# Order of vector work in the first steps of an up-projection: product of g ahead of the weight conversions, a normalisation split in two

## The chip, the cores and the metric

One core of a Trainium2 chip runs the whole program in one launch. The metric is the device time of that launch in microseconds. Three executions of the kernel before took 534.69, 539.32 and 541.73 us; the median, 539.32 us, is what the change is compared with.

The core has four compute engines that matter here, each with its own queue that is worked off in order: PE (TensorE, matrix products), DVE (VectorE), ACT (ScalarE) and POOL (GpSimd). SP (SyncE) issues the transfers. PE writes to PSUM banks; VectorE and ScalarE read them.

## The reference, cut to what matters

```python
attn_out = softmax(scale * q @ k.T + decay, causal) @ v       # 4 batches, 8 heads, 576 tokens, 64 wide
x = attn_out.transpose(0, 2, 1, 3).reshape(2304, 512)
h = x @ w_in                                                  # 512 -> 2048, the up-projection
g = h * (1.0 / (1.0 + np.exp(-h)))
x = g @ w_out
...                                                           # a soft mixture of 8 experts on x
```

The inputs w_in and w_out are float64 in the host's arrays; the kernel reads them as pairs of 32-bit words and turns them into float32 itself.

## The kernel before, in words

The program has three stages: attention (to about 190 us of the profile), the up-projection with everything that hangs on it (about 190 to 480 us), and the tail with the experts.

**The up-projection.** The 2304 tokens are nine chunks of 256 tokens (NCH = 9), the 2048 columns are four groups of 512 (fg = 0 to 3). A step k is one chunk with one group. The first 16 steps take four chunks (NJ = 4) under each group in turn: steps 0 to 3 are group 0, 4 to 7 group 1, and so on; from step 16 the chunks come one after the other. A step has two halves t = 0 and 1 of 128 tokens. Each half is one accumulation of 12 matmuls of 128x512 in one PSUM bank (`h_part`, lines 583 to 601; x and w are each a high and a low part, so lines 593, 594 and 595 follow each other four times). The banks of h are a ring of three (`RINGS["h"] = "014"`): a half can only begin when the half three before it has been read for the last time.

After a half, ScalarE takes its tanh from PSUM (`g_tanh`, line 607, tile gt), and VectorE multiplies (tanh + 1) by h from PSUM (`g_mul`, line 614). This **product of g** is the last reader of the bank, so it is what PE waits for three halves later: the half t = 1 of step k needs the product of the half t = 0 of step k - 1.

**The conversions.** Beside this, VectorE, ScalarE and GpSimd convert the weights that later steps need. A weight block (128x512, tile raw) takes five VectorE instructions (`conv_b` line 486, `conv_d` lines 496, 498, 500, 502), two or three of ScalarE (lines 489, 509, 513) and one or two of GpSimd (line 520 for w_in, lines 524 and 525 for w_out). Blocks go in pairs, so a pair is ten VectorE instructions. `conv_ops(n)` issues from a list (`CQ`, built by `front` and `back`) until n VectorE instructions are out, with those of ScalarE and GpSimd that stand between them. It is called with OPS = 4 twice in every step: between the tanh and the product of the first half, and at the end of the step (one more call ahead of step 0 finds no block to work on). When a pair of w_out is done, its transposes and products (`w_prime_a`, `w_prime_b`, `w_prime_c`, tiles wtp, wp1, wp2) follow on PE in later steps.

**The last normalisation.** The attention output of the last pair of heads is still to be divided by its row sums when the up-projection starts. `norm_b` and `norm_x` (end of step 0) invert the sums, write them to device memory (R) and read them back spread over the partitions (RB, line 334). `norm_c` (lines 338 to 343) then does three VectorE instructions: 128x256 for chunk 6, 128x256 for chunk 7, 128x64 for chunk 8. It stands at the end of step 3. Chunks 6 to 8 are needed much later.

The order on each engine is the order in which the Python code issues (the schedule is manual), so moving a call moves its instructions in the queue.

Of the kernel before, what the change touches and what calls it, by code (L numbers as in the profile page):

```python
# [35 lines left out]
def tile_attention_moe_softmoe(ctx: ExitStack, tc: tile.TileContext, qk, vr, f, wcat, phi, w1, w2, out):  # L36
# [298 lines left out]
                              in_=bass.AP(tensor=r.tensor, offset=r.offset + h * S, ap=[[0, 64], [1, S]]))  # L335
        RT[p] = rb

    def norm_c(p):
        b, hp = divmod(p, NP)
        u, r = U.pop(p), RT.pop(p)  # L340
        for x, c0, n in ((xs[2 * b][:, hp], 0, 256), (xs[2 * b + 1][:, hp], 256, 256),
                         (xs[8][:, hp, 64 * b:64 * b + 64], 512, 64)):
            nc.vector.tensor_tensor(x, u[:, c0:c0 + n], r[:, c0:c0 + n], ALU.mult)

    def att_step(i, cv):
# [206 lines left out]
    def conv_ops(n):  # L552
        while n > 0:
            if not CQ or CQ[0] is None:
                m = mo["todo"]
                more = mo["next"] >= m + 2 and sent[m + 1] + LAG <= mo["k"]
                if CQ:
                    CQ.pop(0)
                    if more:
                        CQ[0:0] = front(m)  # L560
                        CQ.extend(back(m))
                        mo["todo"] += 2
                    continue
                if not more:
                    return
                CQ.extend(front(m) + back(m))
                mo["todo"] += 2
            v, fn, m = CQ.pop(0)
            n -= v
            fn(m)  # L570
# [14 lines left out]
    def h_part(c, fg, t, d0, d1):  # L585
        xh, xl = XC[c]
        if d0 == 0:
            G[c, fg, t] = bank("h", [128, 512], "h")
        o = G[c, fg, t]
        tok = slice(128 * t, 128 * t + 128)  # L590
        for d in range(d0, d1):
            w = W[4 * fg + d]
            nc.tensor.matmul(o, lhsT=xh[:, d, tok], rhs=w[:, 0], start=(d == 0), stop=False)  # L593
            nc.tensor.matmul(o, lhsT=xl[:, d, tok], rhs=w[:, 0], start=False, stop=False)  # L594
            nc.tensor.matmul(o, lhsT=xh[:, d, tok], rhs=w[:, 1], start=False, stop=(d == 3))  # L595
        if t == 1:
            if c == NCH - 1:
                release(*WS[fg][d0:d1])
            if fg == 3 and d1 == 4:
                release(*XS[c])  # L600

    def g_tanh(c, fg, t, parts=1):
        if (c, fg) not in GT:
            GT[c, fg], GS[c, fg] = page([128, 2, 512], "gt")
        n = 512 // parts
        for j in range(parts):
            nc.scalar.activation(GT[c, fg][:, t, n * j:n * j + n], G[c, fg, t][:, n * j:n * j + n], AF.Tanh, scale=0.5)  # L607

    def g_mul(c, fg, t, parts=1):
        n = 512 // parts  # L610
        h = G.pop((c, fg, t))
        for j in range(parts):
            g = GT[c, fg][:, t, n * j:n * j + n]
            nc.vector.scalar_tensor_tensor(g, g, 1.0, h[:, n * j:n * j + n], op0=ALU.add, op1=ALU.mult)  # L614
# [364 lines left out]
    with tc.manual_schedule():  # L979
# [156 lines left out]
        for k, (c, fg) in enumerate(steps):  # L1136
            last = k == len(steps) - 1
            mo["k"] = k
            if k == NJ * 4:
                RINGS.update(h="01", t="254")  # L1140
            if k == STEPS[1]:
                RINGS.update(t="25", g="b4")
            mo["cap"] = [n for at, n in CAPS if k >= at][-1]
            if c == NCH - 1:
                h_part(c, fg, 0, 0, 2)
                h_part(c, fg, 1, 0, 2)
                stacked(k)
                square(k)
                h_part(c, fg, 0, 2, 4)
                g_tanh(c, fg, 0)  # L1150
                g_mul(c, fg, 0)
                h_part(c, fg, 1, 2, 4)
            else:
                h_part(c, fg, 0, 0, 4)
                g_tanh(c, fg, 0)
                conv_ops(OPS)
                g_mul(c, fg, 0)
                halfway(k)
                h_part(c, fg, 1, 0, 4)
            if c in (0, 1) and fg == 0:  # L1160
                split_x(c + 2)
            elif NJ <= c < NCH - 1 and fg == 1:
                split_x(c + 1)
            elif (c, fg) == (NJ - 1, 3):
                split_x(NJ)
            g_tanh(c, fg, 1, 1 + last)
            g_mul(c, fg, 1, 1 + last)
            born[c, fg] = k
            if k == 0:
                norm_b(NPAIR - 1)  # L1170
                norm_x(NPAIR - 1)
            if k == 3:
                norm_c(NPAIR - 1)
                release((xpool, "x1"), (nrm, "U1"), (nrm, "R"))
            if c < NCH - 1:
                stacked(k)
                square(k)
                conv_ops(OPS)
            elif fg != 2:
                stacked(k + 0.5)  # L1180
                if fg == 1:
                    square(k + 0.5)
            if last:
                ct_page(0)
                ct_page(4)
            mo["umax"] = max([0] + [n for at, n in ROOM if k + 1 >= at])
            pump()
# [52 lines left out]
```

## Time and profile before

| | |
|---|---|
| median of three executions | 539.32 us (534.69 to 541.73) |
| profiled execution, its own time | 539.69 us |
| span in the profile, first to last instruction | 538.0 us |
| granted TensorE clock, mean over the span | 0.988 |
| busy share of the span | PE 95%, weight loads 70%, VectorE 62%, ScalarE 55%, GpSimd 39% |

The profile is of one execution. Its times are microseconds from the span's start. The busy shares are averages over stages of very different kind; what the first steps of the up-projection cost has to be read in the stretch from 190 to 300 us. In a row of the timeline, a number in square brackets is the idle time of the engine just before, and behind the arrow stands what ended it.

### The profile page before, as it was taken

To read this page: it belongs to the slowest core of one execution; us is meant where nothing else is said; L and a number is where in the kernel's file an instruction comes from. 1 tells how busy PE (TensorE), PEld (TensorE's weight loads), DVE (VectorE), ACT (ScalarE), POOL (GpSimd) and SP (SyncE) were. 2 spreads that over 40 slices of the span, in tenths; PEclk is the share of its full clock that TensorE was granted. 3 is DMA by queue.
4 is the path that set the end of the run, shared out by engine and by line. 5 is a ranking of instruction groups with operands and counts; after the bars stand their busy time and mean duration, and the time that the engine had idled before them with its cause. 6 is when DMAs were issued, how large, how long until landed. Compare 5 with 4: busy or idle time off the path is not lost.

```text
span 538.0 us, 11312 instructions
## 1 busy us (share of the span) xinstructions
PE 510.0 (95%) x4167; PEld 375.0 (70%) x4167; DVE 332.5 (62%) x891; ACT 296.8 (55%) x585; POOL 208.6 (39%) x228
## 2 busy tenths in 40 slices
PE   8799999999999999899999999999998999999993
PEld 4587787778777777677776777667675667665562
DVE  5747677767789389998888733566654431434023
ACT  8678989888896766456656553323421333341013
POOL 9757888888788404457357300000000000001000
PEclk9989999999999999899999999999999999999997
DMA  5716765576473377212431209789698829767998
GB/s 144 216 66 167 207 197 162 147 216 175 119 191 79 127 295 308 111 40 78 158 100 58 80 1 334 215 240 291 225 340 203 256 69 337 248 256 303 409 396 303
DMA packets 43820, 105.81 MB, mean 197 GB/s; under 512 B 8148, under 2 KB 16628, under 8 KB 43764
## 3 DMA queue, kind: packets, MB, share of 16 engines
q1 hardware_dynamic: 43764, 105.08, 59.8%
q8 instruction: 33, 0.54, 0.4%
q14 instruction: 23, 0.19, 0.1%
HBM read 82.58 MB, written 17.52 MB: 186 GB/s over the span
## 4 chain that ended last, share of the span: by engine, by line
PE 66%; DVE 11%; DMA 9%; ACT 6%; issue 3%; POOL 2%; SPq 1%; DVEq 0%; POOLq 0%; ACTq 0%
PE h L593 9%; PE h L595 8%; PE h L594 8%; PE av L303 4%; PE st L246 4%; PE mx L200 4%; DMA QA<-mr 4%; PE gtp L637 4%; PE st L248 3%; PE lp L664 3%; PE rs L287 3%; PE so L906 3%; PE h L851 3%; PE pp L780 2%; PE st L89 2%
## 5 line engine op out<-in xcount | busy, mean ns | idle before, releaser
L593 PE MATMUL h<-w,xh 128*128 128x512 f32 x288 | 119.3, 414 | 3.7 <-DVE gt L614 3.6
L595 PE MATMUL h<-w,xh 128*128 128x512 f32 x288 | 114.3, 397 | 0.0
L594 PE MATMUL h<-w,xl 128*128 128x512 f32 x288 | 114.1, 396 | 0.0
L614 DVE SCALAR_TENSOR_TENSOR gt<-gt,h 128x512 f32<-128x512 f32 (+1 forms) x73 | 48.4, 674 | 70.0 <-ACT gt L607 70.0
L607 ACT ACTIVATE gt<-h 128x512 f32<-128x512 f32 (+1 forms) x73 | 42.7, 589 | 85.0 <-PE h L595 71.4
L252 ACT ACTIVATE E<-st 128x256 f32<-128x256 f32 (+4 forms) x160 | 63.6, 431 | 15.0 <-PE st L248 12.5
L206 DVE CUSTOM_DVE_ANT_0 junk<-mx,mask 128x64 bf16<-128x64 f32 (+3 forms) x128 | 50.0, 414 | 33.7 <-PE mx L200 32.8
L593 PEld LDWEIGHTS h<-w,xh 128*128 128x128 f32 x288 | 54.6, 189 | 21.4 <-DVE gt L614 7.0
L826 POOL MEMSET SM<- 128x512 f32 x2 | 1.1, 530 | 175.9 <-ACT gt L607 173.3
L595 PEld LDWEIGHTS h<-w,xh 128*128 128x128 f32 x288 | 54.5, 189 | 12.9
L594 PEld LDWEIGHTS h<-w,xl 128*128 128x128 f32 x288 | 54.5, 189 | 11.1
L246 PE MATMUL st<-QA,KA 128*128 128x256 f32 (+2 forms) x192 | 56.4, 304 | 6.0 <-DMA QA<-mr 4.1
L269 POOL TENSOR_SCALAR_AFFINE_SELECT E<-E 128x256 f32<-128x256 f32 (+1 forms) x96 | 41.8, 450 | 28.7 <-ACT E L252 27.3
L248 PE MATMUL st<-QB,KB 128*128 128x256 f32 (+2 forms) x192 | 52.5, 298 | 0.0
L200 PE MATMUL mx<-KA,QA 127*128 127x64 f32 (+2 forms) x192 | 50.6, 330 | 1.8 <-DVE mr L221 0.6
L303 PE MATMUL av<-E,VF 128*64 128x320 f32 (+4 forms) x448 | 50.8, 364 | 0.0
L178 POOL TENSOR_TENSOR QB<-qk,QA 64x576 fp32r<-64x576 f32 x30 | 42.8, 1428 | 2.3
L176 POOL TENSOR_TENSOR KB<-qk,KB 64x576 fp32r<-64x576 f32 x30 | 42.3, 1430 | 1.7 <-ACT KB L170 0.6
L246 PEld LDWEIGHTS st<-QA,KA 128*128 128x128 f32 x192 | 35.1, 183 | 10.6 <-ACT E L252 7.0
L303 PEld LDWEIGHTS av<-E,VF 128*64 128x64 f32 x448 | 29.5, 136 | 17.8 <-POOL E L269 0.3
L524 POOL TENSOR_TENSOR raw<-raw 128x512 f32<-128x512 f32 x16 | 25.4, 1590 | 38.8 <-ACT raw L513 31.8
L200 PEld LDWEIGHTS mx<-KA,QA 127*128 127x128 f32 x192 | 33.4, 192 | 5.9 <-DVE Mt L206 1.8
(155 smaller groups left out, 847.9 us busy)
## 6 DMA issues: line engine op xcount, KB each, us to landing
unit<-in_w_dram SPq DMA_DIRECT2D x64, 512.0 KB
raw<-in_w_dram SPq DMA_DIRECT2D x32, 512.0 KB
far<-gb SPq DMA_DIRECT2D x16, 512.0 KB
gr<-far SPq DMA_DIRECT2D x64, 128.0 KB
qk<-in_qk_dram SPq DMA_DIRECT2D x14, 576.0 KB
VF<-in_v_dram SPq DMA_DIRECT2D x16, 320.0 KB
RB<-R SPq DMA_DIRECT2D x32, 144.0 KB
out_dram<-ob SPq DMA_DIRECT2D x18, 256.0 KB
```

Source lines behind the costliest of these rows:

```text
L178: eng.tensor_tensor(QB.of(p)[64:128, h], src[0:64], QA[p % 3][0:64, h, 64:640], ALU.subtract)
L200: nc.tensor.matmul(t[:, 0:w], lhsT=qa[0:127, h, 128 * blk:128 * blk + 128], rhs=ka[0:127, h, k0:k0 + w], start=True, stop=True)
L206: nc.vector.tensor_tensor_reduce(out=junk[:, 0:w], in0=t[:, 0:w], in1=mask[:, 448 - w:448], scale=1.0, scalar=Mx[p][:, h] if j == 5 else - ...
L246: nc.tensor.matmul(t[0:m, o:o + n], lhsT=ka[:, h, k0:k0 + m], rhs=qa[:, h, 64 + q0:64 + q1], start=True, stop=False)
L248: nc.tensor.matmul(t[0:m, o:o + n], lhsT=kb_[:, h, k0:k0 + m], rhs=qb[:, h, q0:q1], start=False, stop=True)
L252: nc.scalar.activation(e[0:m], t[0:m, 0:o], AF.Exp, scale=0.125)
L303: nc.tensor.matmul(AVP[p][x][64 * h:64 * h + 64, o0:o0 + n], lhsT=VF[p % 2][:, kb, h], rhs=E[2 * p + h][kb][:, c:c + n], start=kb == 0, st ...
L593: nc.tensor.matmul(o, lhsT=xh[:, d, tok], rhs=w[:, 0], start=(d == 0), stop=False)
L594: nc.tensor.matmul(o, lhsT=xl[:, d, tok], rhs=w[:, 0], start=False, stop=False)
L595: nc.tensor.matmul(o, lhsT=xh[:, d, tok], rhs=w[:, 1], start=False, stop=(d == 3))
L607: nc.scalar.activation(GT[c, fg][:, t, n * j:n * j + n], G[c, fg, t][:, n * j:n * j + n], AF.Tanh, scale=0.5)
L614: nc.vector.scalar_tensor_tensor(g, g, 1.0, h[:, n * j:n * j + n], op0=ALU.add, op1=ALU.mult)
```

## The change

Three things move, all in the first steps of the up-projection.

- In steps 0 to 4 the product of the first half stands directly behind its tanh, ahead of the conversions, which come after it. From step 5 the conversions still stand first.
- In steps 1 to 4 each of the two calls of conv_ops issues three VectorE instructions where it issued four. From step 5 the first call issues five and the second four, up to the end of the list.
- The last normalisation is split: its first instruction (chunk 6) stands at the end of step 2, the other two (chunks 7 and 8) at the end of step 3.

```diff
-    def norm_c(p):
+    def norm_c(p, parts=(0, 1, 2)):
...
-        u, r = U.pop(p), RT.pop(p)
+        u, r = U[p], RT[p]
+        for j in parts:
...
                 h_part(c, fg, 0, 0, 4)
+                ops = OPS - (0 < k < 5)
                 g_tanh(c, fg, 0)
-                conv_ops(OPS)
-                g_mul(c, fg, 0)
+                if k < 5:
+                    g_mul(c, fg, 0)
+                conv_ops(ops + (k > 4))
+                if k > 4:
+                    g_mul(c, fg, 0)
                 halfway(k)
                 h_part(c, fg, 1, 0, 4)
...
+            if k == 2:
+                norm_c(NPAIR - 1, (0,))
             if k == 3:
-                norm_c(NPAIR - 1)
+                norm_c(NPAIR - 1, (1, 2))
                 release((xpool, "x1"), (nrm, "U1"), (nrm, "R"))
             if c < NCH - 1:
                 stacked(k)
                 square(k)
-                conv_ops(OPS)
+                conv_ops(ops)
```

No instruction is added or taken away; lines behind 338 shift by one (line 614 is 615 after).

VectorE in the middle of steps 2 and 3, before (tiles gt<-gt,h are the products of g: h_3318 and h_3341 are the two halves of step 2; raw and wt are conversions):

```order
L500 SCALAR_TENSOR_TENSOR raw_3173<-raw_3173 128x512
L500 SCALAR_TENSOR_TENSOR raw_3175<-raw_3175 128x512
L614 SCALAR_TENSOR_TENSOR gt_3331<-gt_3331,h_3318 128x512
L614 SCALAR_TENSOR_TENSOR gt_3331<-gt_3331,h_3341 128x512
L502 TENSOR_SCALAR raw_3173<-wt_3256 128x512
L502 TENSOR_SCALAR raw_3175<-wt_3256 128x512
L496 SCALAR_TENSOR_TENSOR wt_3333<-raw_3177,wt_3333 128x512
L496 SCALAR_TENSOR_TENSOR wt_3333<-raw_3179,wt_3333 128x512
L498 TENSOR_SCALAR raw_3177<-raw_3177 128x512
L498 TENSOR_SCALAR raw_3179<-raw_3179 128x512
L486 TENSOR_SCALAR wt_3391<-raw_3181 128x512
L486 TENSOR_SCALAR wt_3391<-raw_3183 128x512
```

The same place after (h_3316 and h_3336 are the halves of step 2, h_3357 the first half of step 3; x6_100<-UB_103,RB_3247 is the first part of the normalisation):

```order
L615 SCALAR_TENSOR_TENSOR gt_3329<-gt_3329,h_3316 128x512
L499 TENSOR_SCALAR raw_3173<-raw_3173 128x512
L499 TENSOR_SCALAR raw_3175<-raw_3175 128x512
L487 TENSOR_SCALAR wt_3334<-raw_3177 128x512
L615 SCALAR_TENSOR_TENSOR gt_3329<-gt_3329,h_3336 128x512
L344 TENSOR_TENSOR x6_100<-UB_103,RB_3247 128x256
L487 TENSOR_SCALAR wt_3334<-raw_3179 128x512
L501 SCALAR_TENSOR_TENSOR raw_3173<-raw_3173 128x512
L501 SCALAR_TENSOR_TENSOR raw_3175<-raw_3175 128x512
L615 SCALAR_TENSOR_TENSOR gt_3370<-gt_3370,h_3357 128x512
```

Before, the two products of a step stand next to each other with eight conversions to the next two; after, there are three conversions between any two products, and one part of the normalisation stands behind the second product of step 2.

VectorE between the last product of step 4 (h_3447 before, h_3432 after) and the products of step 5 (h_3482 and h_3508 before, h_3452 and h_3476 after), first before:

```order
L614 SCALAR_TENSOR_TENSOR gt_3434<-gt_3434,h_3447 128x512
L486 TENSOR_SCALAR wt_3475<-raw_3185 128x512
L486 TENSOR_SCALAR wt_3475<-raw_3187 128x512
L500 SCALAR_TENSOR_TENSOR raw_3181<-raw_3181 128x512
L500 SCALAR_TENSOR_TENSOR raw_3183<-raw_3183 128x512
L502 TENSOR_SCALAR raw_3181<-wt_3391 128x512
L502 TENSOR_SCALAR raw_3183<-wt_3391 128x512
L496 SCALAR_TENSOR_TENSOR wt_3475<-raw_3185,wt_3475 128x512
L496 SCALAR_TENSOR_TENSOR wt_3475<-raw_3187,wt_3475 128x512
L614 SCALAR_TENSOR_TENSOR gt_3495<-gt_3495,h_3482 128x512
```

and after:

```order
L615 SCALAR_TENSOR_TENSOR gt_3423<-gt_3423,h_3432 128x512
L501 SCALAR_TENSOR_TENSOR raw_3179<-raw_3179 128x512
L503 TENSOR_SCALAR raw_3177<-wt_3334 128x512
L503 TENSOR_SCALAR raw_3179<-wt_3334 128x512
L497 SCALAR_TENSOR_TENSOR wt_3426<-raw_3181,wt_3426 128x512
L497 SCALAR_TENSOR_TENSOR wt_3426<-raw_3183,wt_3426 128x512
L499 TENSOR_SCALAR raw_3181<-raw_3181 128x512
L499 TENSOR_SCALAR raw_3183<-raw_3183 128x512
L487 TENSOR_SCALAR wt_3473<-raw_3185 128x512
L615 SCALAR_TENSOR_TENSOR gt_3465<-gt_3465,h_3452 128x512
L615 SCALAR_TENSOR_TENSOR gt_3465<-gt_3465,h_3476 128x512
```

Here there are eight conversions in either program, but after they are earlier ones of the list: 37 stand between the start of the steps and the product of h_3452, where 44 stood before. From step 6 nine stand between one step's products and the next.

## Rows read from the trace of the kernel before

**Rows 1.** Who waited for whom, 195 to 300 us: us in total, times, longest us

```profile
DVE gt L614 <- ACT gt L607: 5.8, 5, 1.9
...
PE h L593 <- DVE gt L614: 3.3, 2, 2.5
...
DVE wt L486 <- POOL wt L525: 2.3, 1, 2.3
```

**Rows 2.** Timeline of PE: start us, us, engine line, xcount, [idle before <-releaser]

```profile
208.86 0.40 PE L595 MATMUL h<-w,xh 128*128 128x512 f32 x1
210.02 0.50 PE L593 MATMUL h<-w,xh 128*128 128x512 f32 x1 [0.77 <-DVE gt L614]
210.36 0.39 PE L594 MATMUL h<-w,xl 128*128 128x512 f32 x1
210.59 0.40 PE L595 MATMUL h<-w,xh 128*128 128x512 f32 x1
...
221.95 0.40 PE L595 MATMUL h<-w,xh 128*128 128x512 f32 x1
224.88 0.58 PE L593 MATMUL h<-w,xh 128*128 128x512 f32 x1 [2.54 <-DVE gt L614]
...
228.63 0.40 PE L593 MATMUL h<-w,xh 128*128 128x512 f32 x1
...
288.23 0.50 PE L593 MATMUL h<-w,xh 128*128 128x512 f32 x1
```

**Rows 3.** Busy time by stretch: us, PE, PEld, DVE, ACT, POOL, granted clock, DMA share, GB/s

```profile
210.00:220.00 10.00, 9.98 (x47) 8.22 (x48) 10.00 (x17) 4.92 (x9) 7.41 (x4) 1.00 0.82 320
220.00:230.00 10.00, 7.46 (x32) 5.03 (x30) 9.78 (x17) 6.14 (x12) 4.25 (x3) 0.83 0.09 35
```

**Rows 4.** Timeline of VectorE, 190 to 300 us

```profile
192.24 0.90 DVE L343 TENSOR_TENSOR x<-UC,RB 128x256 f32<-128x256 f32 x3 [0.45 <-DMA RB<-R]
...
207.41 0.75 DVE L486 TENSOR_SCALAR wt<-raw 128x512 int32<-128x512 int32 x2
208.08 1.28 DVE L500 SCALAR_TENSOR_TENSOR raw<-raw 128x512 int32<-128x512 int32 x2
209.29 1.27 DVE L614 SCALAR_TENSOR_TENSOR gt<-gt,h 128x512 f32<-128x512 f32 x2
...
213.70 1.28 DVE L614 SCALAR_TENSOR_TENSOR gt<-gt,h 128x512 f32<-128x512 f32 x2
214.90 3.89 DVE L343 TENSOR_TENSOR x<-UB,RB 128x256 f32<-128x256 f32 x3
...
220.59 2.97 DVE L496 SCALAR_TENSOR_TENSOR wt<-raw,wt 128x512 int32<-128x512 int32 x2
...
224.15 1.27 DVE L614 SCALAR_TENSOR_TENSOR gt<-gt,h 128x512 f32<-128x512 f32 x2
...
230.16 0.69 DVE L614 SCALAR_TENSOR_TENSOR gt<-gt,h 128x512 f32<-128x512 f32 x1 [0.38 <-ACT gt L607]
...
271.73 0.69 DVE L614 SCALAR_TENSOR_TENSOR gt<-gt,h 128x512 f32<-128x512 f32 x1 [1.94 <-ACT gt L607]
...
287.50 1.27 DVE L614 SCALAR_TENSOR_TENSOR gt<-gt,h 128x512 f32<-128x512 f32 x2
```

**Rows 5.** Timeline of GpSimd, the first pair of w_out and the pair of w_in behind it

```profile
211.13 3.55 POOL L524 TENSOR_TENSOR raw<-raw 128x512 f32<-128x512 f32 x1 [7.07 <-DVE raw L502]
214.76 1.31 POOL L525 TENSOR_TENSOR wt<-wt,raw 128x512 f32<-128x512 f32 x1
...
220.47 2.55 POOL L520 TENSOR_TENSOR w<-raw 128x512 fp32r<-128x512 f32 x2 [1.76 <-DVE raw L502]
```

**Rows 6.** Groups by line, 196 to 300 us: xcount | busy us, mean ns of one | idle before

```profile
L607 ACT ACTIVATE gt<-h 128x512 f32<-128x512 f32 x30 | 17.5, 591 | 16.8 <-PE h L595 11.4 <-POOL raw L524 2.9 <-issue 2.5
```

**Rows 7.** Timeline of the transfer queue: issue of RB for the last two pairs

```profile
188.70 1.14 SPq L334 DMA_DIRECT2D RB<-R  x2
...
206.56 1.14 SPq L334 DMA_DIRECT2D RB<-R  x2
```

More of the change, by code (lines that the diff above doesn't have):

```diff
@@ L336, in norm_x @@
         RT[p] = rb
-    def norm_c(p):
+    def norm_c(p, parts=(0, 1, 2)):
         b, hp = divmod(p, NP)
-        u, r = U.pop(p), RT.pop(p)
-        for x, c0, n in ((xs[2 * b][:, hp], 0, 256), (xs[2 * b + 1][:, hp], 256, 256),
-                         (xs[8][:, hp, 64 * b:64 * b + 64], 512, 64)):
+        u, r = U[p], RT[p]
+        for j in parts:
+            x, c0, n = ((xs[2 * b][:, hp], 0, 256), (xs[2 * b + 1][:, hp], 256, 256),
+                        (xs[8][:, hp, 64 * b:64 * b + 64], 512, 64))[j]
             nc.vector.tensor_tensor(x, u[:, c0:c0 + n], r[:, c0:c0 + n], ALU.mult)
```

## The prediction

> **What bounds the kernel now.** I read the waits of the stretch first, then PE's timeline at the two places that they name, then the busy shares there, then the timelines of VectorE and GpSimd. By the waits, PE stood still for VectorE's product of g (line 614) twice between 195 and 300 us [rows 1]. PE's timeline shows where, and that the idle time is not the whole price [rows 2]. Matmuls follow each other every 0.23 us (210.36 to 210.59). After 208.86 the next was due at 209.09 and came at 210.02: 0.93 us lost, and the first pitch is 0.34 instead of 0.23: 0.11 more. After 221.95 it was due at 222.18 and came at 224.88: 2.70 us lost. Then nine matmuls fill 224.88 to 228.63, 3.75 us where nine pitches of 0.233 are 2.10: 1.65 us lost at a lower clock; the granted clock of that stretch is 0.83 and that of the one before 1.00 [rows 3], which is time at 1.2 GHz instead of 2.4. Together 0.93 + 0.11 + 2.70 + 1.65 = 5.4 us. These are the half t = 1 of steps 3 and 5, and each began as the product of the step before it ended (the first of the two at 209.29 and at 224.15, each 0.67 us after its start [rows 4]).
>
> Why was the product late? VectorE was busy without a gap: 10.00 of 10 us, then 9.78 [rows 3]. A pair of conversions on it is four instructions at 0.60 us (208.08 to 209.29 for two) and six at 0.34 (207.41 to 208.08 for two) [rows 4], 4.4 us for ten. On top come the three parts of the normalisation, 3.89 us at 214.90 where the same three took 0.90 us at 192.24, and conversions at 220.59 that took 2.97 us for two instead of 1.28 [rows 4]; GpSimd was at work beside both [rows 5]. So in this stretch VectorE sets the pace and PE follows.
>
> The third thing to see is what comes later. At 288.23 PE starts the half t = 1 of step 14 [rows 2], and the product that it needs began at 287.50 and ended 0.68 us later, at 288.18 [rows 4]. There is no slack there: even after the two long waits, PE at step 14 is still let go by VectorE's queue. So PE can be earlier at that point only by as much as VectorE's queue is earlier there. In between VectorE was idle 5.8 us in five waits for a tanh (0.38 us at 230.16 the first, 1.94 at 271.73 the last) and once 2.3 us for GpSimd [rows 1, 4].
>
> **The change, part by part, as a ledger of VectorE's queue up to 288.18.** No instruction is added or removed, so what can change is work done by then, idle time, and time lost beside GpSimd.
>
> Conversions moved back. Up to the product of step 5's first half 44 conversions stand before, 37 after: seven fewer are 3.4 us by their kinds. Steps 3 and 5 gain that (six and ten fewer, 2.5 and 4.4 us, at the products that let them go), so by work alone the waits at 209 and 222 us go: 2.5 covers 0.93, and 4.4 covers 2.70 and the lost clock. But from step 5 one more stands in each step, and up to the product of step 13's first half it is 109 against 108. The ledger at 288.18 gets +0.6 us (one instruction of 0.60), not a gain.
>
> Idle time that can be squeezed out. The five waits for a tanh are the only place from which PE's earlier arrival can be paid: tanh comes earlier if PE does. At most all 5.8 us go, at least none. A queue that is to lose all its idle time would have to be at work 100% over 60 us while its inputs come in lumps; I take 40%, 2.3 us.
>
> Idle time that is new. In steps 0 to 4 ten products stand closer behind their tanh: three conversions lie between products where eight did. What hid the tanh before was the conversions between; ahead of the first product of a step there are now three of them, 1.0 to 1.8 us. VectorE works in order, so behind a product that waits everything waits, the conversions that ScalarE needs among them, and the next tanh stands in ScalarE's queue behind those. A tanh takes 0.59 us [rows 6]. Bounds: nothing, or 0.59 for each of ten, 5.9 us. I take half, 3.0 us, near what the shortest and longest of the seen waits (0.38, 1.94) suggest for some of the ten.
>
> The normalisation. Its three instructions cost between 0.90 and 3.89 us [rows 4], so splitting them is worth between -3.0 and 0 us. GpSimd's four instructions of that pair come at the same place of the list, so I take 0. The first part also gets a wait: it stands at the end of step 2 and needs RB. For the pair before, 3.5 us passed from the issue at 188.70 [rows 7] to its use at 192.24 [rows 4]; from the issue at 206.56 [rows 7] that gives 210.1. VectorE would be there at about 208.9 (the second product of step 2 began 0.6 us after 209.29; less 1.5 us for three conversions fewer ahead of it, plus 0.6 for itself), so it may idle 1.2 us; behind it stand conversions and the first product of step 3, due by 214.7, so PE feels nothing at once. It is one of the new idles and lies within the 3.0.
>
> What else moves: the transposes and products of the first w_out pairs on PE come one step later, as many as before; weights of groups 2 and 3 come up to a step later and are needed steps after; the transfers of raw blocks follow the buffers. None sets an end, since the transfer engines are nearly idle between 220 and 230 us (share 0.09 [rows 3]).
>
> How GpSimd gets in is a question of its own. At 211.13 its instruction was issued and took 3.55 us, while VectorE ran the six conversions that stand behind line 502 in the order shown; it ended 0.98 us after a product of g had begun at 213.70 [rows 4, 5]. At 220.59 each conversion waited: 2.97 less 1.28 is 1.7 us for two, 0.85 each. The Trainium skill, "SBUF — State Buffer", section "Who interferes with whom", says that VectorE and GpSimd lock a shared pair of ports for a whole instruction, the one issued first having it, and that a VectorE instruction with at most one operand in SBUF and outside the two-port modes (the product of g, whose h lies in PSUM) does not take it. The trace agrees that a product lets GpSimd in; it disagrees that the first issued goes first, since conversions issued after 211.13 went ahead. By that rule products that stand apart let GpSimd in sooner and more often: a rival below.
>
> **The sum.** At 288.18: +0.6 (work) - 2.3 (squeezed) + 3.0 (new idle) + 0 (normalisation) = +1.3 us. The lost clock does not enter, since PE is paced by VectorE anyway. After step 14 the two programs agree within two conversions, and the rest shifts with PE. The profiled execution took 539.69 us, 1.7 more than its span and 0.4 above the median: 539.7 + 1.3 = 541.0 us.
>
> **The rivals.**
> - *All is gained.* The idle time is squeezed out and the normalisation escapes GpSimd: up to 3.0 + 5.8 - 0.6 = 8.2 us shorter in the queue, but PE has only its 5.4 us to gain: 534.3 us. For it: every product that the two waits hung on has 2.5 to 4.4 us less before it. Against it: no slack at 288.23.
> - *Slower.* One mechanism: VectorE waits at each product that now stands close behind its tanh in steps 0 to 4. Nothing is squeezed and the full 5.9 us are lost: +0.6 + 5.9 = +6.5, 546.2 us. Place: the idle time in front of line 615 up to step 5. It decides from the point where new idle exceeds the 3.4 us that the product of step 5 wins; from there steps 6 to 10 have waits longer than those that went.
> - *GpSimd gets in sooner.* Two more collisions at 0.85 us each on top of the forecast, +1.7: 542.7 us. For it the 3.55 us, during which VectorE lost nothing; against it that the number of GpSimd's instructions is the same. By the page's rule the whole of it would be so.
>
> **How the numbers follow.** Forecast 541.0 with 0.45 (its own range 538.5 to 543.5), all gained 0.27, slower 0.18, GpSimd 0.10. What a measurement of this kernel can tell from no change is about 2%, 10.8 us; none of the cases reaches it: faster by over 2% 0.01, within 2% 0.97, slower 0.02. The range runs from a little under the gain, 533.8, to the slower case, 546.5.
>
> **What would show it.** Right: the waits of PE at steps 3 and 5 are gone, PE waits again for line 615 in steps 6 to 11, VectorE idles in front of products in steps 0 to 4, and the start of step 14's second half lies within 3 us of 288.2. Wrong: PE runs steps 3 to 14 with no wait for line 615 and step 14 begins 5 us earlier (all gained), or new waits of VectorE for the tanh sum to more than 3.4 us.

## The result, and the profile after

| | kernel before | changed kernel |
|---|---|---|
| median of 20 executions each, side by side | 538.83 us (533.95 to 542.24) | 541.65 us (538.31 to 544.59) |
| ratio, 95% interval | | 1.0059 (1.0039 to 1.0079) |
| profiled execution, own time and span | 539.69 and 538.0 us | 538.9 and 537.2 us |

The change makes the kernel 0.4 to 0.8% slower, some 3 us: less than the 2% that counts as a difference here, but on one side. The forecast was 541.0 us, within 2%, with a small loss.

The profiled execution of the changed kernel happens to be among its faster ones: it left the attention earlier. To compare the two profiles I therefore measure from one instruction that both have and that only little of the change precedes on VectorE: line 318, behind the products of step 0. It starts at 198.37 us before and at 194.50 after (in the fourteen profiles of this case anywhere from 192.6 to 198.9). From there to the end of the span it is 339.6 us before and 342.7 after, +3.1 us, near the 2.8 us of the medians. These are single executions: in e1 to e3 below, whose medians are those of the kernel before, this stretch is 338.5 to 341.0 us.

The waits of the changed kernel between 195 and 300 us (total us, times, longest), against [rows 1]:

```profile
PE h L594 <- DVE gt L615: 4.9, 3, 2.6
DVE gt L615 <- ACT gt L608: 2.6, 4, 0.9
DVE wt L487 <- POOL wt L526: 2.3, 1, 2.3
PE gtp L638 <- ACT wT L677: 1.4, 2, 1.1
```

PE waits longer for the product of g than before (4.9 us against 3.3), VectorE less for the tanh (2.6 against 5.8), and there is a longer wait for ScalarE's copy of a transposed block (1.4 us, in all 0.6 before). PE's timeline, against [rows 2]:

```profile
216.49 0.50 PE L594 MATMUL h<-w,xh 128*128 128x512 f32 x1 [0.39 <-DVE gt L615]
...
225.18 0.51 PE L594 MATMUL h<-w,xh 128*128 128x512 f32 x1 [1.95 <-DVE gt L615]
...
240.44 0.63 PE L594 MATMUL h<-w,xh 128*128 128x512 f32 x1 [2.61 <-DVE gt L615]
240.86 0.63 PE L595 MATMUL h<-w,xl 128*128 128x512 f32 x1
...
244.19 0.40 PE L594 MATMUL h<-w,xh 128*128 128x512 f32 x1
...
260.21 1.03 PE L638 MATMUL gtp<-ident,gt 128*128 128x128 f32 x7 [1.09 <-ACT wT L677]
...
286.38 0.40 PE L594 MATMUL h<-w,xh 128*128 128x512 f32 x1
```

The three waits are the second halves of steps 5, 6 and 8: the one of step 3 is gone, that of step 5 shrank to 0.39 us, and two new ones came. Behind the last, nine matmuls fill 240.44 to 244.19, 3.75 us where nine pitches of 0.233 are 2.10: the lower clock again, 1.65 us lost, as much as before. So PE stood idle 0.39 + 1.95 + 2.61 = 4.95 us, where it had stood 0.77 + 2.54 = 3.31 [rows 2]; one more first pitch of 0.34 adds 0.11 and the wait for the copy some 0.8. Together that is some 2.5 us more, and 2.0 of it are still there at the second half of step 14: it starts at 286.38, which is 91.9 us behind line 318; before it was 288.23 - 198.37 = 89.9. In e1 to e3 it is 89.2 to 90.4. The busy shares, against [rows 3] (PE, PEld, DVE, ACT, POOL, granted clock, DMA share, GB/s):

```profile
220.00:230.00 10.00, 8.05 (x41) 5.74 (x40) 10.00 (x19) 7.15 (x13) 4.81 (x3) 1.00 0.01 2
230.00:240.00 10.00, 7.83 (x36) 6.09 (x34) 10.00 (x12) 4.41 (x9) 7.12 (x6) 1.00 0.29 105
240.00:250.00 10.00, 9.56 (x39) 7.75 (x40) 9.95 (x16) 6.17 (x11) 5.67 (x4) 0.83 0.16 50
```

VectorE is full from 220 to 250 us, later than before. Between 230 and 240 us it finishes only 12 instructions in 10 us, where it finishes 19 in the stretch ahead of it. Its timeline shows why, against [rows 4]:

```profile
189.53 0.69 DVE L615 SCALAR_TENSOR_TENSOR gt<-gt,h 128x512 f32<-128x512 f32 x1 [0.39 <-ACT gt L608]
...
194.50 0.17 DVE L318 TENSOR_SCALAR sg<-sg 96x12 f32<-96x12 f32 x1
...
206.14 0.43 DVE L344 TENSOR_TENSOR x<-UB,RB 128x256 f32<-128x256 f32 x1
...
210.66 1.92 DVE L344 TENSOR_TENSOR x<-UB,RB 128x256 f32<-128x256 f32 x2
...
218.66 0.69 DVE L615 SCALAR_TENSOR_TENSOR gt<-gt,h 128x512 f32<-128x512 f32 x1 [0.95 <-ACT gt L608]
...
229.74 1.28 DVE L615 SCALAR_TENSOR_TENSOR gt<-gt,h 128x512 f32<-128x512 f32 x2
230.94 2.62 DVE L487 TENSOR_SCALAR wt<-raw 128x512 int32<-128x512 int32 x2
233.49 2.40 DVE L501 SCALAR_TENSOR_TENSOR raw<-raw 128x512 int32<-128x512 int32 x2
235.81 0.75 DVE L503 TENSOR_SCALAR raw<-wt 128x512 int32<-128x512 int32 x2
236.48 2.97 DVE L497 SCALAR_TENSOR_TENSOR wt<-raw,wt 128x512 int32<-128x512 int32 x2
...
239.71 1.27 DVE L615 SCALAR_TENSOR_TENSOR gt<-gt,h 128x512 f32<-128x512 f32 x2
...
284.90 1.44 DVE L615 SCALAR_TENSOR_TENSOR gt<-gt,h 128x512 f32<-128x512 f32 x2
```

and GpSimd's, against [rows 5]:

```profile
230.80 1.30 POOL L526 TENSOR_TENSOR wt<-wt,raw 128x512 f32<-128x512 f32 x1
232.06 1.23 POOL L525 TENSOR_TENSOR raw<-raw 128x512 f32<-128x512 f32 x1
233.36 1.37 POOL L526 TENSOR_TENSOR wt<-wt,raw 128x512 f32<-128x512 f32 x1
236.36 2.54 POOL L521 TENSOR_TENSOR w<-raw 128x512 fp32r<-128x512 f32 x2 [1.63 <-DVE raw L503]
```

Nine conversions stand between two pairs of products (229.74 and 239.71), and five GpSimd instructions start in that stretch. By these times the two engines take turns: two conversions that take 0.75 us when nothing is beside them (235.81) take 2.62, two that take 1.28 take 2.40 and 2.97. Nine conversions that are 4.1 us by their kinds take 8.8 (230.94 to 239.71).

For the whole stretch from line 318 to the product of step 13's first half (287.50 before, 284.90 after; 89.1 and 90.4 us), VectorE's instructions grouped by line (times, busy us, mean ns, idle before them). Before:

```profile
L496 DVE SCALAR_TENSOR_TENSOR wt<-raw,wt 128x512 int32<-128x512 int32 x20 | 17.3, 901 | 0.0
L614 DVE SCALAR_TENSOR_TENSOR gt<-gt,h 128x512 f32<-128x512 f32 x25 | 16.5, 678 | 5.8 <-ACT gt L607 5.8
L500 DVE SCALAR_TENSOR_TENSOR raw<-raw 128x512 int32<-128x512 int32 x20 | 14.2, 749 | 0.0
...
L486 DVE TENSOR_SCALAR wt<-raw 128x512 int32<-128x512 int32 x22 | 11.3, 555 | 2.3 <-POOL wt L525 2.3
```

and after:

```profile
L497 DVE SCALAR_TENSOR_TENSOR wt<-raw,wt 128x512 int32<-128x512 int32 x20 | 21.1, 1087 | 0.0
L615 DVE SCALAR_TENSOR_TENSOR gt<-gt,h 128x512 f32<-128x512 f32 x25 | 16.6, 679 | 1.9 <-ACT gt L608 1.8
L501 DVE SCALAR_TENSOR_TENSOR raw<-raw 128x512 int32<-128x512 int32 x21 | 14.7, 735 | 0.0
...
L487 DVE TENSOR_SCALAR wt<-raw 128x512 int32<-128x512 int32 x22 | 13.4, 640 | 2.3 <-POOL wt L526 2.3
```

One conversion more (L501, 21 against 20), idle time in front of the products down from 5.8 to 1.9 us, and the same conversions longer: L497 by 3.8 us and L487 by 2.1. On VectorE that is what the change does; the experiments ask why the two last nearly cancel.

### The profile page after: what moved, and what is told of

Same layout as the page of the kernel before. It is cut to its first block, busy times and chain, and to the rows that moved or that the text cites. A ratio compares the mean times of both kernels' runs of the same rounds, so it can differ in the third digit from the quotient of the medians.

```text
span 537.2 us, 11308 instructions
## 1 busy us (share of the span) xinstructions
PE 508.3 (95%) x4167; PEld 373.9 (70%) x4167; DVE 336.5 (63%) x891; ACT 295.7 (55%) x585; POOL 207.1 (39%) x228
## 4 chain that ended last, share of the span: by engine, by line
PE 62%; DVE 14%; DMA 9%; ACT 7%; issue 3%; SPq 2%; POOL 2%; DVEq 0%; ACTq 0%; POOLq 0%
PE h L594 8%; PE h L596 7%; PE h L595 7%; PE av L303 5%; PE st L246 4%; PE mx L200 4%; PE gtp L638 3%; PE st L248 3%; PE lp L665 3%; DMA gr<-far 3%; PE rs L287 3%; PE pp L781 3%; PE so L907 3%; DVE wt L497 3%; PE h L852 3%
## 5 line engine op out<-in xcount | busy, mean ns | idle before, releaser
L525 POOL TENSOR_TENSOR raw<-raw 128x512 f32<-128x512 f32 x16 | 23.3, 1455 | 34.6 <-ACT raw L514 31.0
```

## The experiments

To compare them, one ledger for every run. VectorE's **own work** from line 318 to the product of step 13's first half is 62.3 us in the kernel before: of 104 conversions 40 at 0.60 and 64 at 0.335 us (the pitches of [rows 4]), 24 products at 0.60, and 2.5 us for the rest. The **time** is the distance of those two rows on VectorE's timeline. The **rest** is time less work: idle time, and **held** time, in which an instruction takes longer than its pitch, as it does beside GpSimd. The ratio is against the kernel before on the same chip. Work, time and rest are read from one execution each.

| run | work | time | rest | ratio (95%) |
|---|---|---|---|---|
| before | 62.3 | 89.1 | 26.8 | 1 |
| changed | 62.9 | 90.4 | 27.5 | 1.0059 (1.0039 to 1.0079) |
| e1 products ahead alone | 62.3 | 88.5 | 26.2 | 0.9991 (0.9966 to 1.0016) |
| e2 three conversions alone | 62.9 | 88.6 | 25.7 | 1.0004 (0.9980 to 1.0028) |
| e3 split normalisation alone | 62.3 | 89.7 | 27.4 | 0.9998 (0.9977 to 1.0020) |
| e4 later catch-up | 63.9 | 93.0 | 29.1 | 1.0188 (1.0148 to 1.0228) |
| e5 no GpSimd for w_out | 62.9 | 77.5 | 14.6 | 0.9907 (0.9881 to 0.9933) |
| e6 line 486 three times | 73.4 | 98.3 | 24.9 | 1.0198 (1.0161 to 1.0234) |
| e7 changed, products first always | 61.0 | 92.8 | 31.8 | 1.0173 (1.0137 to 1.0209) |
| e8 before, products first always | 61.0 | 89.2 | 28.2 | 1.0065 (1.0036 to 1.0094) |
| f1 before, w_out multiplied by VectorE | 69.5 | 89.2 | 19.7 | 1.0001 (0.9971 to 1.0031) |
| f2 changed, w_out multiplied by VectorE | 70.1 | 90.2 | 20.1 | 1.0040 (1.0016 to 1.0065) |
| f3 before, w_in and w_out by VectorE | 74.3 | 91.3 | 17.0 | 0.9990 (0.9968 to 1.0012) |
| f4 as f3, transposes a step later | 74.3 | 86.1 | 11.8 | 0.9893 (0.9848 to 0.9938) |

### The three parts, each alone, and the catch-up

e1, in the kernel before:

```diff
                 g_tanh(c, fg, 0)
+                if k < 5:
+                    g_mul(c, fg, 0)
                 conv_ops(OPS)
-                g_mul(c, fg, 0)
+                if k > 4:
+                    g_mul(c, fg, 0)
```

e2, in the kernel before:

```diff
+                ops = OPS - (0 < k < 5)
                 g_tanh(c, fg, 0)
-                conv_ops(OPS)
+                conv_ops(ops + (k > 4))
                 g_mul(c, fg, 0)
...
-                conv_ops(OPS)
+                conv_ops(ops)
```

e3, in the kernel before (norm_c as in the changed kernel):

```diff
+            if k == 2:
+                norm_c(NPAIR - 1, (0,))
             if k == 3:
-                norm_c(NPAIR - 1)
+                norm_c(NPAIR - 1, (1, 2))
```

e4, in the changed kernel:

```diff
-                conv_ops(ops + (k > 4))
+                conv_ops(ops + (k > 7))
...
-                conv_ops(ops)
+                conv_ops(ops + (k > 7))
```

> The kernel before with one part of the change alone: in steps 0 to 4 the product of the first half stands ahead of the conversions (four conversions a call everywhere, normalisation in one). Theory (VectorE and GpSimd together pace the stretch up to step 14, and the order only moves the waits): within 0.3% of before, the idle time of VectorE in front of products in steps 0 to 4 under 2 us. Rival A (the products that stand close behind their tanh are what costs): 0.4 to 0.8% slower than before, new waits of VectorE for the tanh of over 3 us.

> The kernel before with another part alone: three conversions a call in steps 1 to 4, five and four a step from step 5, products behind the conversions, normalisation in one. Theory (moved conversions come back and meet GpSimd later): 0.2 to 0.6% slower than before, PE's waits for the product of g lie in steps 5 to 9 instead of 3 and 5. Rival A (the products ahead are the cost): within 0.2% of before. Rival B (fewer conversions early is a gain that the rest of the change loses): 0.3 to 0.8% faster.

> The kernel before with the normalisation in two parts alone, the first at the end of step 2. In the changed kernel the three parts took 2.4 us where they took 3.9 before. Theory: a saving of VectorE's queue of up to 1.5 us ahead of step 5, so at best 0.3% faster and within 0.3% in any case. Rival (the first part waits for its transfer and holds the first product of step 3 back): 0.2 to 0.5% slower, with an idle time of VectorE in front of line 344.

> The changed kernel with the fifth conversion of a step taken back later: four and four in steps 5 to 7, five and five from step 8. Theory (VectorE's queue and GpSimd pace the stretch up to step 14, the total is the same): within 0.25% of the changed kernel, so 0.3 to 0.8% slower than before; the waits at steps 6 and 8 become smaller and one in steps 9 to 12 appears. Rival B (the catch-up from step 5 is what costs): at the time of before or faster, and PE waits for a product of g less than 2 us in all.

No part alone makes a difference that shows: each interval has 1 in it. Each moves PE's waits elsewhere without taking them away. e2 has a single one of 2.61 at the second half of step 8, e3 two (3.9 us, the longest 3.1), and e1 five short ones, as its waits between 196 and 300 us say:

```profile
PE h L593 <- DVE gt L614: 3.6, 5, 1.1
```

The granted clock of e1 stayed at 1.00 in the three stretches from 210 to 240 us, so it paid nothing at a lower clock. VectorE's waits for a tanh are 2.8 us there, 1.0 of them in steps 2 and 4, so rival A falls too. The expectation for e2 (0.2 to 0.6% slower) was too dark, though its waits came where it said. e2 also shows where the new wait for the copy of a transposed block comes from: it is there at 1.1 us (1.5 in all), and in e1 and e3 the total is 0.6 as before, so it belongs to the conversions that are moved back. In e3 the first part of the normalisation waited 0.28 us for RB, and the rival (0.2 to 0.5% slower) falls.

The three ratios multiply to 0.999 (0.995 to 1.003, if their intervals are independent), the three parts together measured 1.0059 (1.0039 to 1.0079). So the loss is, by a small margin, one of the parts together; which pair of them makes it was not tried. The traces narrow it down. VectorE's timeline of e2 has the same held conversions between the products of steps 6 and 7 as the changed kernel has at 230.94:

```profile
231.46 2.62 DVE L486 TENSOR_SCALAR wt<-raw 128x512 int32<-128x512 int32 x2
234.01 2.40 DVE L500 SCALAR_TENSOR_TENSOR raw<-raw 128x512 int32<-128x512 int32 x2
...
237.00 2.97 DVE L496 SCALAR_TENSOR_TENSOR wt<-raw,wt 128x512 int32<-128x512 int32 x2
```

So they, and PE's wait of 2.61 us behind them, come from the conversions moved back, and in e2 they cost nothing in all. What the changed kernel has beyond e2 are the waits of 0.39 and 1.95 us at steps 5 and 6.

e4 was to move the cost and multiplied it: theory and rival both missed. The product of step 13 comes 93.0 us behind line 318 (197.34), 2.6 us later than in the changed kernel (VectorE's timeline of e4):

```profile
290.30 0.67 DVE L615 SCALAR_TENSOR_TENSOR gt<-gt,h 128x512 f32<-128x512 f32 x1
```

Only two conversions more than there stand ahead of it, 0.9 us of work. The waits of PE in e4 between 196 and 300 us are now of other kinds too, beside 4.8 us for products of g:

```profile
PE wp L694 <- ACT small L685: 3.9, 1, 3.9
PE gtp L638 <- ACT wT L677: 3.9, 1, 3.9
```

ScalarE's copies stand in its queue behind activations that wait for conversions, and with ten conversions a step they wait long: the copy `small` at 299.36 stands behind one that waited 4.46 us for line 501 (ScalarE's timeline). Here conversions that are put off have a price outside VectorE.

### Who sets the pace: GpSimd's instructions taken away, VectorE's added

e5, in the changed kernel (the low part of w_out is left out of the computation):

```diff
-            nc.gpsimd.tensor_tensor(lo, lo, hi, ALU.mult)
-            nc.gpsimd.tensor_tensor(t, t, lo, ALU.add)
```

e6, in the kernel before, line 486 twice more:

```diff
         nc.vector.tensor_scalar(t, hi, 9, 0x3FFFFF, ALU.logical_shift_right, ALU.bitwise_and)
+        if mo["todo"] and mo["k"] > 6:
+            nc.vector.tensor_scalar(t, hi, 9, 0x3FFFFF, ALU.logical_shift_right, ALU.bitwise_and)
+            nc.vector.tensor_scalar(t, hi, 9, 0x3FFFFF, ALU.logical_shift_right, ALU.bitwise_and)
```

> The changed kernel without the two GpSimd instructions of each w_out block (the low part of w_out is left out of the computation). Theory P (PE paces from step 9 on and never makes good what it waits earlier; the waits come from VectorE's conversions being held beside GpSimd): PE's waits for the product of g in steps 3 to 8 fall from 4.9 us to under 1 us, the stretch up to step 14 is 5 to 7 us shorter than in the changed kernel, 0.5 to 1.0% faster than before. Rival G (VectorE's own instructions are the load and GpSimd hardly matters): the waits stay over 3 us and the time lies within 0.3% of the changed kernel, 0.3 to 0.8% slower than before.

> The kernel before, with line 486 issued three times instead of once from step 7 on (12 blocks, 24 instructions more of 0.34 us, 8 us of VectorE's queue, the same values). Theory V (that of the prediction: VectorE's queue paces up to step 14, without slack there): the product of step 13 comes 4 to 8 us later and the time is 0.7 to 1.5% longer. Theory P (PE paces from step 9 on, VectorE has 8 us of idle time there): the product of step 13 comes less than 2 us later and the time is within 0.4% of before.

e6 decides between V and P, and for V, with more than it asked: 1.98% slower. Its instructions write the same tile one after the other, and each of the 24 adds 0.46 us instead of 0.335, also with no GpSimd instruction beside it (249.09 to 250.35: 0.45, 0.46 and 0.34), so the 24 are 11.1 us of work. The product of step 13 came at 294.09, 98.3 us behind line 318 (195.82) and 9.2 us later than before (VectorE's timeline of e6):

```profile
294.09 0.68 DVE L617 SCALAR_TENSOR_TENSOR gt<-gt,h 128x512 f32<-128x512 f32 x1
```

The reader is to see what did not happen. VectorE had 8.1 us of idle time in this stretch (5.8 and 2.3, above) and it is nearly all gone in e6, whose waits between 196 and 300 us are:

```profile
PE h L596 <- DVE gt L617: 11.9, 6, 3.6
...
DVE gt L617 <- ACT gt L610: 0.2, 1, 0.2
```

but taking it away hid only 2 of the 11.1 us. The other 6 us of the idle time came back as conversions held beside GpSimd, in line 499 for one (496 before), in the groups of e6 up to that product:

```profile
L499 DVE SCALAR_TENSOR_TENSOR wt<-raw,wt 128x512 int32<-128x512 int32 x20 | 22.3, 1156 | 0.0
```

1156 ns against 901. That fits this reading: in VectorE's idle time GpSimd works without holding it up, and whoever fills that time sends GpSimd into the conversions. The rest in the table hardly moves, 24.9 to 27.5 us in six versions that keep GpSimd's list and give VectorE from 62.3 to 73.4 us of work, while its two parts trade places: idle time of 8.1, 7.8, 5.1, 5.0, 4.1 and 0.2 us (before, e3, e1, changed, e2, e6) goes with held time of 18.7, 19.6, 21.1, 22.5, 21.6 and 24.7. (e4, and e7 and e8 below, have 28.2 to 31.8: they put waits of another kind on top.)

e5 is the counter-test: with 24 of GpSimd's 32 instructions out of the stretch, the rest falls by 13 us against the changed kernel and the held time in it from 22.5 to 5.0, no wait of PE for a product of g is left, and VectorE waits 18.9 us for a tanh (waits of e5 between 196 and 300 us):

```profile
DVE gt L613 <- ACT gt L606: 18.9, 12, 5.9
```

0.93% faster than before, 5 us, near what the prediction worked out for PE to gain (5.4), though the product of step 13 comes 12 us earlier. Rival G falls.

### The product first in every step

```diff
                 g_tanh(c, fg, 0)
-                if k < 5:
-                    g_mul(c, fg, 0)
+                g_mul(c, fg, 0)
                 conv_ops(ops + (k > 4))
-                if k > 4:
-                    g_mul(c, fg, 0)
```

(e7 in the changed kernel; e8 is the same order in the kernel before, with four conversions a call.)

> The changed kernel with the product of the first half ahead of the conversions in every step, not only in steps 0 to 4. Theory P: the waits of the changed kernel lie in steps 6 and 8, just behind the place where the conversions come first again; with them behind the product everywhere PE waits under 1.5 us for products of g and the time is 0.4 to 1.0% shorter than before. Theory V (VectorE's queue paces, its work is the same): the waits go elsewhere, within 0.3% of the changed kernel, 0.3 to 0.9% slower than before.

> The kernel before with the product of the first half ahead of the conversions in every step, and nothing else changed (four conversions a call, normalisation in one). Theory P: the two last of the four waits that the version with the products ahead in steps 0 to 4 alone kept (at steps 6 and 7, 0.80 and 1.13 us) go, 0.2 to 0.7% shorter than before. Theory V: within 0.2% of before.

Theory P, by which it is enough to have the product early, falls here for good: 1.7 and 0.65% slower. V is missed too: by it e7 lay within 0.3% of the changed kernel and e8 within 0.2% of the kernel before. What happens is the prediction's slower rival, only not in the changed kernel. VectorE waits at product after product behind its tanh, the conversions behind wait too, ScalarE waits for them, and PE waits for ScalarE's copies. The waits of e7 between 196 and 300 us:

```profile
DVE gt L615 <- ACT gt L608: 9.6, 11, 2.5
PE gtp L638 <- ACT wT L677: 5.4, 1, 5.4
```

### Fewer turns for GpSimd, with nothing left out

Since GpSimd's instructions cost VectorE so much, let VectorE do the multiplication itself. One instruction does ScalarE's scaling (line 513) and GpSimd's product (line 524 or 520) at once:

```diff
+            out = lo if kind else W[fi][:, 1]
+            nc.vector.scalar_tensor_tensor(out, raw[:, :, 0], 2.0 ** -35, hi, op0=ALU.mult, op1=ALU.mult)
...
-            nc.gpsimd.tensor_tensor(lo, lo, hi, ALU.mult)
```

(f1 for w_out in the kernel before, f2 the same in the changed kernel, f3 for w_out and w_in in the kernel before. The scaling on ScalarE goes.) f4 is f3 with

```diff
-            stage[0] = mo["wp"].pop(0)[1] if mo["wp"] and mo["wp"][0][0] < k - bool(CQ) else None
+            stage[0] = mo["wp"].pop(0)[1] if mo["wp"] and mo["wp"][0][0] < k - bool(CQ) - (k < 5) else None
```

> The kernel before, with the multiplication of the low part of each w_out block taken from GpSimd (1.3 us and more) and its scaling from ScalarE (0.6 us) and both done by one VectorE instruction (0.60 us); GpSimd keeps the addition. Same result. Theory (what VectorE loses beside GpSimd, collisions and idle together some 27 us up to step 13, follows GpSimd's work): VectorE's work grows by some 7 us and the 27 us fall by 9 to 13, PE's waits for the product of g fall from 3.3 us to under 1.5, 0.3 to 0.9% faster than before. Rival (VectorE's own instructions are the load, a queue that gets 7 us more is 7 us later): 0.7 to 1.5% slower.

> The same replacement in the changed kernel. Theory: with fewer GpSimd instructions to meet, the order of the first steps matters less: within 0.3% of the same replacement in the kernel before, 0.3 to 0.9% faster than before. Rival (VectorE's own instructions are the load): 1.2 to 2.0% slower than before.

> The kernel before, with the replacement for the w_in blocks too, so that GpSimd keeps only the additions of w_out. Eight more instructions of 0.60 us on VectorE (4.8 us), eight fewer of 1.25 us on GpSimd. Theory: the exchange goes on paying as long as VectorE still collides, within 0.3% of the version for w_out alone, faster than before by 0.3 to 1.0%. Rival (VectorE's own instructions are the load): 1.2 to 2.5% slower than before.

> The kernel before with the low parts of w_in and w_out multiplied by VectorE, and in steps below 5 the transposes of a finished w_out pair one step later, so that PE no longer meets GpSimd's late addition at the end of step 4 (4.0 us in the version without this). Same result. Theory (VectorE, freed of GpSimd, has slack; PE lost only that one wait and half clock behind it): PE waits under 1.5 us in all in steps 0 to 14, the product of step 13 comes 4 us or more earlier than in that version, 0.5 to 1.0% faster than before. Rival V (VectorE's queue of some 89 us up to step 13 holds whatever PE does): the wait comes back as one for the product of g, within 0.3% of before.

f1 to f3 kept the first half of what the theory said and missed the second. VectorE got 7 to 12 us more work and was little later or not at all (89.2 and 90.2 us in f1 and f2, 91.3 in f3; the rival's 0.7 to 2.5% slower falls). The rest fell to 17 to 20 us, in f1 by 7 us, not the 9 to 13 expected. Held time follows the number of GpSimd's instructions in the stretch: 18.7 us with 32 (before), 10.0 with 20 (f1), 4.7 with 12 (f3). The waits for a product of g fell to 0.7 and 0.3 us in f1 and f3 (f2: 3.2). But the time stayed, and in f1 and f3 PE met another wait (2.8 us in f1). The waits of f3 between 196 and 300 us:

```profile
PE wtp L683 <- POOL wt L533: 4.0, 1, 4.0
...
PE h L601 <- DVE gt L622: 0.3, 1, 0.3
```

and GpSimd's timeline there:

```profile
206.28 11.12 POOL L533 TENSOR_TENSOR wt<-wt,raw 128x512 f32<-128x512 f32 x2 [25.75 <-DVE raw L523]
```

Two additions took 11.12 us on GpSimd. The transposes of that w_out pair stand at the end of step 4 and waited 4 us for them. f4 moves these transposes one step, and then little is in the way: 0.9893 (0.9848 to 0.9938), PE's waits for a product are 1.4 us (with those for copies 2.8, where under 1.5 was expected), and the product of step 13 comes 86.1 us behind line 318, 5.2 us earlier than in f3. It is a little faster than the 0.5 to 1.0% expected.

f4 has the median 532.7 us, beside 537.84 for the kernel before on that chip: faster than both kernels of this case, with the whole computation done. The later transposes without VectorE's products were not tried, and the scaling on ScalarE goes too, so f4 does not say how much each of them gives. In f2 the order of the first steps seems to cost still (1.0040, f1 has 1.0001; the intervals overlap), with 12 of GpSimd's 32 instructions gone; its expectation is missed on both counts.

## Why the prediction was right, and where its terms were off

The number was right, 541.0 against 541.65 us, and so was its frame: what one part wins, VectorE's queue takes back. The sum at the product of step 13 was forecast at +1.3 us and measured at 90.4 - 89.1 = +1.3. That the two agree to a tenth is luck: e1 to e3, as fast as the kernel before, have 88.5 to 89.7 in the same place, and the +1.3 came out of terms of which two were well off and one was missing. The nearness of 541.0 is in part luck too, since the forecast stands on a profiled execution of 539.69, 0.9 us above the median of twenty.

**Work, +0.6.** Right: one conversion more (L501 in the groups above).

**Idle time squeezed out, -2.3, and new idle time, +3.0.** Both mis-sized, and the prediction put them together at +0.7. Measured, all idle time fell by 3.1 us, from 8.1 to 5.0 (5.8 and 2.3 before; 1.9 and 2.3 after, and 0.7 for xh and 0.1 elsewhere). Of the 5.8 us in front of products 0.8 are left (at steps 10 and 11), so 5.0 were squeezed out. New are 0.95 us for a tanh at 218.66 and the 0.7 for xh, 1.7 in all; one more wait for a tanh, 0.39 us at 189.53 in step 0, lies ahead of line 318. For the other products three conversions in between were cover enough; the full price of 0.59 us for each of ten products is not paid. e7 shows where it is paid: 9.6 us, when the product stands first in every step.

**Time beside GpSimd, taken at 0.** This is the term that was wrong. The forecast put nothing down for it, and the rival that did set two collisions at 0.85 us, +1.7. Of the ledger's rest of 27.5 us, 5.0 is idle, so 22.5 is held time; before, 26.8 less 8.1 is 18.7. So +3.8 us. By the two tables of groups L497 and L487 alone took 5.9 us more than before; against that stand above all 1.5 us of the normalisation (0.43 at 206.14 and 1.92 at 210.66, where the three parts took 3.89 [rows 4]). That is twice the rival's price, but not by the rival's mechanism, products that stand apart and let GpSimd in sooner. GpSimd did get in sooner at its first w_out pair (1.60 us at 209.44 where it had taken 3.55 [rows 5]), but up to the product of step 5 VectorE was held only 0.9 us longer than before. The other 3.0 us lie behind it, where the two products of a step stand together again: 4.7 us between the products of steps 6 and 7 (8.8 less 4.1, above) against 0.5 before. e2, with its products behind the conversions, has the same there, and e1, with the products ahead, 0.5.

The two errors cancelled. To the tenth that is luck; that they work against each other is not, as e6 and the six versions with nearly the same rest show. Idle time of VectorE and its held time behave as one account: GpSimd's instructions have to stand somewhere, beside products, in idle time, or in the way. Squeezing idle time out, the prediction's one source of gain, was worth almost nothing in the versions that keep GpSimd's list.

**The normalisation, 0 within -3.0 to 0.** It got 1.5 us shorter; by itself (e3) it is worth nothing. In the changed kernel's profile the first part did not wait for RB at all; in e4 and e7, which have the same order there, it waited 1.0 us, near the 1.2 that the prediction allowed for.

**What else moves, "none sets an end".** Not quite: the transposes that come a step later bring the wait for ScalarE's copy, some 0.8 us (e2 has it too).

**No slack at 288.23.** Half right. In the kernel before PE began 0.05 us after the product had ended, 0.47 us behind the matmul ahead of it (287.76) where the pitch is 0.23, so the product did let it go; and e6 shows how tight VectorE's queue was: given more, it sets the pace to the end. In the changed kernel PE came to that place at 286.38, 0.8 us after the product had ended (284.90 and 0.68): no wait for a product came behind that of step 8, and PE carried on what it had lost until then, and at the copy. The two accounts come near each other, +1.3 on VectorE and +2.0 on PE.

**Size.** The forecast's +1.3 on 539.7 is a ratio of 1.0024, below the measured interval. What is missing is behind step 13: +2.0 instead of +1.3 at step 14, and a wait of PE for transfers (gr) that was 3.0 us in all before and 3.8 after. Those are 1.5 of the 1.8 us between +1.3 and the +3.1 from line 318 to the end.

**The signs named ahead.** The wait at step 3 went, that at step 5 nearly; new waits came in steps 6 and 8, inside the band of 6 to 11; step 14's second half lies within 3 us. VectorE's idle time in front of products in steps 0 to 4 came twice, 0.39 us at 189.53 and 0.95 at 218.66.

The rival "all is gained" failed for the reason given against it, and e5 and f4 show that its size was right: 5 us are to be had, but with GpSimd's instructions taken out of VectorE's way, not by this order.

## What to carry to other kernels

Before you count an engine's idle time as room, look who works in it: where VectorE and GpSimd take turns, filling VectorE's gaps mostly moves GpSimd into its instructions. Keep a ledger of work and rest to one fixed instruction: if the rest stays while the order changes, look for what the rest is made of, and take that away. A freed engine shows the next wait at once (here the transposes in f3), so read the waits again before calling an idea void.

## What was not expected of the hardware

**How GpSimd gets in depends on what VectorE is at.** At 230.80 a GpSimd instruction began beside a product of g (the second of the two at 229.74). From there three of them in a row had their turn, 1.23 to 1.37 us each from 230.80 to 234.73, with a conversion held about 1 us every time. In f4 the first of two additions began beside a conversion, at 208.34. The two took 4.20 and 6.96 us, one directly behind the other, and VectorE beside them lost nothing; each ended together with a pair of products (at 211.28 and 218.24). GpSimd's timeline of f4, the durations (least, median, most, in ns), and VectorE's timeline:

```profile
208.34 11.12 POOL L533 TENSOR_TENSOR wt<-wt,raw 128x512 f32<-128x512 f32 x2 [25.75 <-DVE raw L523]
```

```profile
L533 POOL TENSOR_TENSOR wt<-wt,raw x2: 4195/5578/6962, 208.3 to 212.5; 128x512 f32<-128x512 f32 x2
```

```profile
208.73 1.28 DVE L496 SCALAR_TENSOR_TENSOR wt<-raw,wt 128x512 int32<-128x512 int32 x2
...
211.28 1.27 DVE L622 SCALAR_TENSOR_TENSOR gt<-gt,h 128x512 f32<-128x512 f32 x2
...
218.24 1.27 DVE L622 SCALAR_TENSOR_TENSOR gt<-gt,h 128x512 f32<-128x512 f32 x2
```

The 3.55 us at 211.13 in the kernel before end beside a pair of products too (213.70) [rows 4, 5]. That the product is what lets GpSimd in fits all of these; no run tests it by itself.

The Trainium skill, "SBUF — State Buffer", section "Who interferes with whom", has the pair of ports locked for one instruction at a time; the turns at 230 us agree with that. That the instruction issued first goes first does not: conversions issued long after 208.34 went ahead of an addition that had been issued.

**One VectorE instruction for two.** Multiplying an int32 operand by a number and then by a float32 operand takes 0.60 us for 128x512, as the conversions of that form do (1.29 for two in f1, in the row at 211.38), in place of 0.6 on ScalarE and at least 1.04 on GpSimd (line 524 between 196 and 300 us: 1.04 at the least, 1.23 in the median).

**The granted clock.** It was 1.00 in the stretch with PE's wait of 1.95 us at 225.18 and 0.83 in the stretch behind the wait of 2.61 at 240.44, with eight matmuls at the pitch of 1.2 GHz. In e1 five waits of up to 1.13 us left it at 1.00: in these executions the same VectorE queue cost PE less when it was late in small pieces.
